# Moving the third plain tile of the first unit of block products

## The chip, the cores and the metric

The kernel runs on one core of one Trainium2 chip. The metric is the device time of one execution in microseconds, lower is better; times are medians over runs. Engines are named as in the profile: PE (TensorE), DVE (VectorE), ACT (ScalarE), POOL (GpSimd), SP (SyncE, here a queue of transfers), and PEld for the loading of PE's weights.

## The reference

Three stages follow one another, all in float32:

```
x = attention(q, k, v)              # 2 x 8 heads x 768 x 64 -> x: 1536 x 512
P = sinkhorn(exp(x @ w_gate))       # 8 rounds, P: 1536 x 8
for e in range(8):                  # dense mixture of experts, F = 1024
    out += P[:, e:e+1] * (relu(x @ w1[e]) @ w2[e])
out2 = routed mixture of experts(out)   # one expert of 8 for each row
```

The change lies in the second stage, the dense mixture.

## The kernel before

**Numbers in two parts.** Each float32 operand of a matmul is kept as two parts, `hi` (a cast, written by ACT) and `lo` (the rest, a subtraction on DVE). A product takes three matmuls: hi x hi, hi x lo, lo x hi.

**The dense stage.** An expert is cut into two halves of 512 features, `hx` = 0 to 15. The first two halves (`hx` 0 and 1) go the plain way in units of 384 rows: `mm1` (L597) makes the features and `mm2` (L624) adds one tile of 128 rows to its accumulator, in 12 matmuls of 512 columns; this is a plain tile. From `hx` = `FIRST` = 2 on, both layers are done as seven block products instead of eight on sets of 512 rows (`self.sets`, three for each `hx`). `first` (L747) gives the seven products of layer one, `s1` to `s7`, and `second` (L846) those of layer two, `z1` to `z7`, which use the features of the set before. So layer two runs one unit behind layer one. Each product is 12 matmuls of 256 columns at L708 (`multiply`), and yields twice, once ahead of each half.

**The order of a unit** is written by hand:

```python
TURNS = "s1 z1 s2 z7 z6 s6 s7 z5 s5 z2 z4 s3 z3 s4".split()
```

The first unit of block products (`hx` 2, set 0) has no layer two behind it (`behind` is None), so its z turns are free. Three plain tiles of `hx` 1 are still waiting then (rows 1152 to 1535, tiles 9, 10 and 11), and `pieces` puts them and some beats into the free turns. In what follows, tile A, B and C are the first, second and third of them; the unit after the first is called the second unit.

**Beats.** At every yield `steps` (L942) calls `beats` (L512) once. A beat first takes one step of every chain that is under way (`self.soon`) and then pops one entry of the list `self.later`. So the place of small work on DVE, ACT and POOL is counted in beats. A chain with None between its steps spreads them over beats. The engines run their instructions in the order in which they are issued here.

**The weights of layer two.** When no plain tile is left, `tiles` (inside `pieces`) issues `rescale` for tiles 9, 10 and 11 (L649 on POOL, then a store at L652 on SP) and calls `new_seconds(2)`. This fills `self.later` with, in order,

```
B11, sumT1, sumT3, T3, sumT2, T2, T1, B21, sumT4, T4, B22
```

each followed by a None, then one more None, and then four loads of the next layer-one weights (L466, on POOL's queue). So entry 0 is B11, entry 6 T3, entry 10 T2, entry 12 T1, entry 20 B22, and entries 23 to 26 are the loads. A `sum` entry is one DVE instruction (L575). Each other entry is the cast `hi` on ACT (L590) in its beat and the subtraction `lo` on DVE (L591) two beats later. Product z1 uses B11, z7 uses T3, z6 uses T2, z5 uses T1. The buffers of the raw weights number four, and the loads reuse them.

**Work behind the products.** Product s5 is followed by a copy of its PSUM bank X on ACT (L802), then on later beats an addition on DVE (L803), a relu and a cast on ACT, a subtraction on DVE. Product s3 adds to the same bank X, so its first matmul waits for that copy. After s3, DVE runs L809 and L810 at once and L818 and three subtractions (L743) on later beats; after s4, L840 at once, and L739, L837 and one L743 on later beats. After s2, DVE runs L782. Results of layer two leave through POOL as adding transfers to memory (L886).

**Transfers of SP.** The right-hand operands T of layer one are read back from memory into a ring of seven; after each of s6, s7, s5 and s4 the next one is fetched (L534, two transfers on SP's queue). SP's stores of `rescale` are in the same queue.

Of the kernel before, what the change touches and what calls it, by code (L numbers as in the profile page):

```python
# [387 lines left out]
class DenseMoe:  # L388
# [612 lines left out]
    def pieces(self, done, plain):  # L1001

        NG = self.NG
        self.seen = set()
        units = [(hx, g) for hx in range(self.FIRST) for g in range(NG)] + self.sets  # L1010
        waiting, behind = [], None
        soon = range(self.FULL + 1, self.LAST)

        def loads(which, hx):
            return [partial(self.load, which, hx, c) for c in range(4)]

        def new_seconds(hx):

            if hx <= self.FULL:
                for what in self.SECONDS:  # L1020
                    self.later += [partial(self.weights, 2, hx, what), None]
                self.later += [None] + loads(1, hx + 1)
            elif hx < self.LAST:
                for what in self.SECONDS_SOON:
                    if what is None:
                        self.later.append(None)
                    elif isinstance(what, int):
                        self.later.append(partial(self.load, 1, hx + 1, what))
                    else:
                        self.later.append(partial(self.weights, 2, hx, what))  # L1030
            else:
                for what in self.SECONDS:
                    self.later += [partial(self.weights, 2, hx, what), None]
                self.later += [None] + loads(1, hx + 1)

        def tiles(hx, n=1):

            for _ in range(min(n, len(waiting))):
                e, i, f = waiting.pop(0)
                yield  # L1040
                yield from f()
                if not waiting and (2, hx, 0) in self.raw:
                    if hx == self.FIRST:
                        for t in range(3 * NG - 3, 3 * NG):
                            self.rescale(t)
                        new_seconds(hx)
                    else:
                        self.later += [partial(self.split, 2, hx, c) for c in range(4)]

        for u, self.goal in self.opening():  # L1050
            yield u
        waiting = self.left
        for i, (hx, g) in enumerate(units):
            if i < NG - 1:
                continue
            n = hx + 1
            last = i + 1 == len(units) or units[i + 1] == (n, 0)
            if self.strassen(hx):
                self.blocks = {}
                todo = {**self.first(hx, g), **(behind or {})}  # L1060
                for k, turn in enumerate(self.TURNS):
                    if turn in todo:
                        for _ in todo[turn]():
                            yield i
                        if (hx, g) == (self.FIRST, 0) and k == 0:
                            for t in range(3 * NG - 3):
                                self.rescale(t)
                    elif turn in ("z1", "z7", "z6"):
                        for _ in tiles(hx):
                            yield i  # L1070
                    elif turn in ("z2", "z4"):
                        self.beats()
                        self.beats()
                    if last and n > self.LAST:
                        if turn in ("s7", "s5", "s3", "s4"):
                            self.split(1, n, ("s7", "s5", "s3", "s4").index(turn))
                    elif last:
                        for what in (self.FIRSTS_LATE if hx in soon else self.FIRSTS).get(turn, ()):
                            self.weights(1, n, what)
                    if last and hx == self.FULL:  # L1080
                        for c in {"s5": (0,), "z3": (1, 2)}.get(turn, ()):
                            self.load(2, n, c)
                        if turn == "s4":
                            self.later += [None, None, partial(self.load, 2, n, 3)]
                    elif last and turn == "s4":
                        self.later += [None] + loads(2, n)
                    if g == 0 and behind and turn == ("z1" if hx in soon else "z6"):
                        new_seconds(hx)
                behind = self.second(hx, g, self.blocks)
                continue  # L1090
            for c in range(4):
                yield i
                if g == 1 and n <= self.FIRST:
                    self.load(1, n, c)
                for _ in self.mm1(hx, g, c):
                    yield i
                if last and self.strassen(n):
                    for turn in (("s1", "s2", "s6", "s7"), ("s5",), ("s3",), ("s4",))[c]:
                        for what in self.FIRSTS[turn]:
                            self.weights(1, n, what)  # L1100
                    if c == 3:
                        self.later += loads(2, n)
                elif last:
                    self.split(1, n, c)
                    self.load(2, n, c)
                for _ in tiles(hx, 1 + (len(waiting) + c > 3)):
                    yield i
            waiting = self.tiles_of_group(hx, g)
        yield from self.rest(len(units), behind, loads, done, plain)
# [1248 lines left out]
```

## Time and profile before

| | |
|---|---|
| median of 3 runs | 1288.38 us (1287.43 to 1289.87) |
| the profiled execution, its own time | 1287.23 us |
| its span in the profile | 1285.5 us |
| mean granted clock of PE | 0.997 |
| busy PE, DVE, ACT, POOL | 99%, 69%, 61%, 29% of the span |

Times in the rows are microseconds from the start of the span. The span is the stretch from the first to the last instruction, and the time lies 1.73 us above it. PE is the engine that is busy nearly all the time. The first unit of block products runs on PE from 213.53 to 232.65 us, the second from 232.65 us on.

### The profile page before, as it was taken

To read this page: it belongs to the slowest core of one execution; us is meant where nothing else is said; L and a number is where in the kernel's file an instruction comes from. 1 tells how busy PE (TensorE), PEld (TensorE's weight loads), DVE (VectorE), ACT (ScalarE), POOL (GpSimd) and SP (SyncE) were. 2 spreads that over 40 slices of the span, in tenths; PEclk is the share of its full clock that TensorE was granted. 3 is DMA by queue.
4 is the path that set the end of the run, shared out by engine and by line. 5 is a ranking of instruction groups with operands and counts; after the bars stand their busy time and mean duration, and the time that the engine had idled before them with its cause. 6 is when DMAs were issued, how large, how long until landed. Compare 5 with 4: busy or idle time off the path is not lost.

```text
span 1285.5 us, 27044 instructions
## 1 busy us (share of the span) xinstructions
PE 1267.0 (99%) x10187; PEld 1194.1 (93%) x10187; DVE 885.4 (69%) x1724; ACT 782.5 (61%) x1601; POOL 376.6 (29%) x388
## 2 busy tenths in 40 slices
PE   7999999999999999999999999999999999999997
PEld 7888898999999999999999999999999978888886
DVE  7754596777778686777877777778697677514261
ACT  5764322667767676776776767767677635425361
POOL 6652005323324242333332323323122201211110
PEclk9999999999999999999999999999999999999999
DMA  9950237778889797988888989889897648123450
GB/s 224 195 123 10 91 120 274 198 193 184 191 189 194 197 201 172 218 171 224 165 211 185 199 191 185 190 189 199 194 213 177 144 150 303 58 73 134 150 182 23
DMA packets 172220, 221.20 MB, mean 172 GB/s; under 512 B 46927, under 2 KB 103279, under 8 KB 172080
## 3 DMA queue, kind: packets, MB, share of 16 engines
q1 hardware_dynamic: 119504, 146.20, 37.1%
q0 software_dynamic: 52576, 73.19, 33.3%
q8 instruction: 82, 1.34, 0.4%
q14 instruction: 58, 0.48, 0.1%
HBM read 163.76 MB, written 56.36 MB: 171 GB/s over the span
## 4 chain that ended last, share of the span: by engine, by line
PE 91%; DMA 3%; issue 2%; DVE 1%; ACT 1%; POOL 1%; POOLq 0%; SPq 0%; DVEq 0%; ACTq 0%
PE bank L708 62%; PE bank L1960 9%; PE bank L631 7%; PE bank L611 5%; DMA out_dram<-o,r_idxf 3%; PE bank L687 2%; PE bank L223 1%; PE bank L292 1%; PE bank L1989 1%; PE bank L279 1%; DMA kn<-in_k_dram 1%; PE bank L1236 0%; PE bank L1951 0%; PE bank L103 0%; ACT e L252 0%
## 5 line engine op out<-in xcount | busy, mean ns | idle before, releaser
L886 POOL DMA_DIRECT2D x2d<-acc x156 | 187.1, 1241 | 502.7 <-DVE lo L591 179.1
L708 PE MATMUL bank<-hi,hlo 128*128 128x256 f32 x748 | 211.5, 283 | 0.3 <-DVE hlo L743 0.3
L708 PE MATMUL bank<-lo,hhi 128*128 128x256 f32 x748 | 211.4, 283 | 0.0
L708 PE MATMUL bank<-hi,hhi 128*128 128x256 f32 x748 | 211.0, 282 | 0.0
L708 PE MATMUL bank<-Tlo,hi 128*128 128x256 f32 x640 | 181.0, 283 | 0.0
L708 PE MATMUL bank<-Thi,lo 128*128 128x256 f32 x640 | 180.7, 282 | 0.0
L708 PE MATMUL bank<-Thi,hi 128*128 128x256 f32 x640 | 180.1, 281 | 0.0
L708 PE MATMUL bank<-hi,acc 128*128 128x256 f32 x744 | 147.9, 282 | 0.0
L708 PEld LDWEIGHTS bank<-hi,hhi 128*128 128x128 f32 x748 | 142.4, 190 | 0.3 <-DVE Thi L906 0.2
L708 PEld LDWEIGHTS bank<-hi,hlo 128*128 128x128 f32 x748 | 141.8, 190 | 0.5 <-DVE hlo L743 0.5
L708 PEld LDWEIGHTS bank<-lo,hhi 128*128 128x128 f32 x748 | 141.8, 190 | 0.1
L708 PE MATMUL bank<-xhi,hi 128*128 128x256 f32 x480 | 134.9, 281 | 0.7 <-ACT t L802 0.7
L708 PE MATMUL bank<-xlo,hi 128*128 128x256 f32 x480 | 134.9, 281 | 0.0
L708 PE MATMUL bank<-xhi,lo 128*128 128x256 f32 x480 | 134.8, 281 | 0.0
L708 PEld LDWEIGHTS bank<-hi,acc 128*128 128x128 f32 x744 | 121.5, 190 | 0.0
L708 PEld LDWEIGHTS bank<-Thi,hi 128*128 128x128 f32 x640 | 121.1, 189 | 0.0
L708 PEld LDWEIGHTS bank<-Thi,lo 128*128 128x128 f32 x640 | 120.6, 188 | 0.0
L708 PEld LDWEIGHTS bank<-Tlo,hi 128*128 128x128 f32 x640 | 120.3, 188 | 0.0
L743 DVE TENSOR_TENSOR hlo<-t,hhi 128x512 fp32r<-128x512 f32 x160 | 107.9, 686 | 15.0 <-ACT hhi L735 13.5
L735 ACT CAST hhi<-t 128x512 fp32r<-128x512 f32 x160 | 97.8, 619 | 28.4 <-DVE t L837 21.9
L881 ACT ACTIVATE acc<-acc,P 128x256 f32<-128x256 f32 x234 | 104.7, 501 | 2.0 <-DVE acc L923 2.0
L708 PE MATMUL bank<-lo,acc 128*128 128x256 f32 x372 | 105.1, 283 | 0.0
(337 smaller groups left out, 3233.3 us busy)
## 6 DMA issues: line engine op xcount, KB each, us to landing
x2d<-acc POOLq DMA_DIRECT2D x163, 256.0 KB, 4.7
Thi<-td SPq DMA_DIRECT2D x160, 256.0 KB, 3.7
Tlo<-td SPq DMA_DIRECT2D x160, 256.0 KB, 4.2
raw<-in_moe_w_dram POOLq DMA_DIRECT2D x88, 256.0 KB, 5.8
raw<-in_moe_w_dram SPq DMA_DIRECT2D x20, 1024.0 KB, 5.9
raw<-in_moe_w_dram SPq DMA_DIRECT2D x56, 256.0 KB, 4.5
vw<-in_v_dram SPq DMA_DIRECT2D x32, 120.0 KB, 4.5
kn<-in_k_dram SPq DMA_DIRECT2D x8, 384.0 KB, 5.2
```

The source lines that it names most:

```text
L223: nc.tensor.matmul(self.sc[par][64 * hh:64 * hh + 64, j, slice(96, 120) if own else slice(0, 96)], qT[p, 64 * t:64 * t + 64], ks[p] if own ...
L279: nc.tensor.transpose(tr[0:120, j, :], an[:, 3 * par + j, :], self.ident)
L292: nc.tensor.matmul(o[64 * par:64 * par + 64, 128 * j + 64 * hh:128 * j + 64 * hh + 64], vw[:, t, par, :], aT[:, 3 * par + j, 64 * hh:64 * ...
L611: nc.tensor.matmul(ps, w[:, 128 * k:128 * k + 128], x[:, k], start=(n == 0), stop=(n == 11),)
L631: nc.tensor.matmul(ps, h, w, start=(n == 0), stop=(n == last))
L687: nc.tensor.matmul(ps, w[:, 128 * k:128 * k + 128], x[:, k], start=(n == 0), stop=(n == 11))
L708: self.nc.tensor.matmul(bank[:, 256 * f:256 * f + 256], x[:, o:o + 128], y[:, k], start=first and n == 1, stop=n == 12, skip_group_check=True,
L735: nc.scalar.copy(hi, src)
L743: nc.vector.tensor_tensor(out=lo, in0=src, in1=hi.bitcast(F32), op=ALU.subtract)
L881: nc.scalar.activation(out=out[:, s], in_=src[:, s], func=ACTF.Copy, scale=self.P[:, i, hx // 2:hx // 2 + 1],)
L886: nc.gpsimd.dma_start(out=self.sums[n:n + 256, 256 * dh:256 * dh + 256].rearrange("(c p) d -> p c d", p=128), in_=out.rearrange("p (c d) - ...
L1960: self.nc.tensor.matmul(ps, x[:, k], y[:, k], start=(n == 0), stop=(n == 12 * len(parts) - 1))
```

## The change

Tile C moves from turn z6, ahead of s6, to turn z4, between s5 and s3. The four extra beats, which stood together at z2 and z4 between s5 and s3, are now two at z6 (where tile C was) and two at z2, ahead of tile C. In the turns of the first unit:

```
before: s1 A s2 B C       s6 s7 s5 2+2 beats   s3 s4
after:  s1 A s2 B 2 beats s6 s7 s5 2 beats  C  s3 s4
```

With tile C, what its end sets off moves too: `rescale` of tiles 9 to 11 with its stores, and `new_seconds(2)`. In all other units every z turn holds a product, so nothing changes there.

```diff
@@ -1065,10 +1065,10 @@
                         if (hx, g) == (self.FIRST, 0) and k == 0:
                             for t in range(3 * NG - 3):
                                 self.rescale(t)
-                    elif turn in ("z1", "z7", "z6"):
+                    elif turn in ("z1", "z7", "z4"):
                         for _ in tiles(hx):
                             yield i
-                    elif turn in ("z2", "z4"):
+                    elif turn in ("z6", "z2"):
                         self.beats()
                         self.beats()
                     if last and n > self.LAST:
```

## Rows read from the trace of the kernel before

**Rows 1.** The page: busy time, share of the span and instructions of each engine.
```profile
PE 1267.0 (99%) x10187; PEld 1194.1 (93%) x10187; DVE 885.4 (69%) x1724; ACT 782.5 (61%) x1601; POOL 376.6 (29%) x388
```

**Rows 2.** Waits of PE, 200 to 300 us: total, times, longest.
```profile
PE bank L708 <- ACT t L802: 0.7, 1, 0.7
PE bank L708 <- DVE hlo L743: 0.3, 1, 0.3
```

**Rows 3.** Timeline of PE, first and second unit: start, duration, instruction, [idle before].
```profile
221.81 0.39 PE L631 MATMUL bank<-hi,hhi 128*128 128x512 f32 x1
...
224.53 0.28 PE L708 MATMUL bank<-Thi,hi 128*128 128x256 f32 x1
...
228.72 0.28 PE L708 MATMUL bank<-Thi,lo 128*128 128x256 f32 x1
229.67 0.39 PE L708 MATMUL bank<-xhi,hi 128*128 128x256 f32 x1 [0.68 <-ACT t L802]
229.89 0.28 PE L708 MATMUL bank<-xlo,hi 128*128 128x256 f32 x1
...
236.90 0.29 PE L708 MATMUL bank<-hi,hhi 128*128 128x256 f32 x1
...
238.34 0.28 PE L708 MATMUL bank<-hi,hhi 128*128 128x256 f32 x1
...
239.05 0.39 PE L708 MATMUL bank<-hi,hlo 128*128 128x256 f32 x1 [0.31 <-DVE hlo L743]
239.27 0.28 PE L708 MATMUL bank<-hi,hhi 128*128 128x256 f32 x1
...
240.35 0.28 PE L708 MATMUL bank<-Thi,hi 128*128 128x256 f32 x1
```

**Rows 4.** Timeline of DVE, first and second unit.
```profile
226.66 0.98 DVE L575 TENSOR_TENSOR raw<-raw 128x512 f32<-128x512 f32 x1
...
230.25 0.68 DVE L591 TENSOR_TENSOR lo<-raw,hi 128x512 fp32r<-128x512 f32 x1
...
232.30 0.68 DVE L809 SCALAR_TENSOR_TENSOR t<-bank,t 128x512 f32<-128x512 f32 x1
...
233.50 0.68 DVE L591 TENSOR_TENSOR lo<-s,hi 128x512 fp32r<-128x512 f32 x1
...
240.24 0.68 DVE L782 TENSOR_TENSOR t<-bank,t 128x512 f32<-128x512 f32 x1
```

**Rows 5.** Timeline of ACT, the copy of bank X behind s5.
```profile
229.03 0.59 ACT L802 COPY t<-bank 128x512 f32<-128x512 f32 x1 [2.28 <-PE bank L708]
```

**Rows 6.** Timeline of POOL, 205 to 290 us.
```profile
225.51 2.46 POOL L649 TENSOR_SCALAR acc<-acc,P 128x512 f32<-128x512 f32 x1 [1.16 <-DVE acc L638]
...
243.03 0.72 POOL L466 DMA_DIRECT2D raw<-in_moe_w_dram  x1 [3.96 <-DVE lo L591]
248.15 1.25 POOL L886 DMA_DIRECT2D x2d<-acc  x1 [4.40 <-DMA Thi<-td]
...
276.25 3.35 POOL L466 DMA_DIRECT2D raw<-in_moe_w_dram  x4
```

**Rows 7.** Timeline of SP's queue, the stores of `rescale`.
```profile
220.25 8.07 SPq L652 DMA_DIRECT2D x2d<-acc  x3
```

**Rows 8.** Timeline of DVE, third unit and after: sums of loaded weights.
```profile
255.46 0.68 DVE L575 TENSOR_TENSOR s<-raw 128x512 f32<-128x512 f32 x1
...
284.37 0.69 DVE L575 TENSOR_TENSOR raw<-raw 128x512 f32<-128x512 f32 x1 [0.75 <-DMA raw<-in_moe_w_dram]
```

**Rows 9.** Stretches: length, busy PE, PEld, DVE, ACT, POOL, clock, DMA, GB/s.
```profile
13.30:16.10 2.80, 0.07 (x3) 0.04 (x2) 2.69 (x16) 1.89 (x8) 1.07 (x1) 0.88 1.23 213
...
15.00:20.00 5.00, 3.91 (x36) 3.44 (x40) 2.91 (x15) 2.68 (x13) 3.79 (x4) 0.66 1.25 219
...
1277.00:1278.00 1.00, 0.41 (x2) 0.00 (x0) 0.00 (x0) 0.56 (x1) 0.00 (x0) 1.00 0.00 0
...
1281.00:1282.00 1.00, 0.00 (x0) 0.00 (x0) 0.00 (x0) 0.00 (x0) 0.00 (x0) 0.90 0.02 4
```

## The prediction

> **What bounds the kernel now.** I read the page first: PE is busy 99% of the span [rows 1], so time is won or lost only where PE waits or where a matmul is added, and this change adds none. Next the waits of PE around the first unit: between 200 and 300 us there are just two, 0.7 us for a copy on ACT and 0.3 us for a subtraction on DVE [rows 2]. The timeline of PE then shows where they lie [rows 3]. The first is in the first unit between s5 and s3: s5's last matmul starts at 228.72, s3's first should follow 0.12 later and starts at 229.67, and its second, due at 228.96, starts at 229.89. That is a loss of 0.93 us. It is the copy of bank X behind s5, which runs from 229.03 to 229.62 [rows 5]. The second is in z6 of the second unit: its third matmul starts at 239.05 and its fourth at 239.27 instead of 238.70, a loss of 0.57 us; the operand is the subtraction for block S2. Last the timeline of DVE: from L809 (232.30) to L782 (240.24) it runs 13 steps in 7.94 us, 0.61 us each, without a hole [rows 4]. In that stretch DVE is the engine that is behind, and PE lives from what was done earlier.
>
> **What the change gains.** Without the hole the end of s5, 228.84, becomes the end of tile C, because the same pieces stand before it. Tile C takes 2.72 us (221.81 to 224.53), so s5 ends at 226.12 and s3 begins at 228.84. The copy on ACT starts 0.19 us after the end of s5 (229.03 against 228.84) and takes 0.59, so it is done at 226.9, 1.9 us ahead of s3. The gain is 0.93 us. What hides the copy is tile C, which uses another bank. Everything on PE after it comes 0.93 us earlier unless something new is late.
>
> **What it delays.** `new_seconds` is called at the end of tile C. Before, 14 beats of the first unit followed it (s6, s7, s5 two each, four extra, s3 and s4 two each); now four follow (s3 and s4). So every entry of the list comes ten beats, or five products, later against the products that use it. Before, B11, sumT1 and sumT3 ran on DVE until 227.64 and T3's `lo` at 230.25 [rows 4], in time that DVE had free. Now B11 is cast at s3, its `lo` and sumT1 come at s4, sumT3 at the second unit's s1, T3's cast at z1 and its `lo` at s2, one product ahead of z7 that reads it; sumT2 comes at s2, T2's cast at z7 and its `lo` at z6, in the very product that reads it. So these six DVE steps move into the stretch in which DVE had no hole.
>
> The queue of DVE, written out in the new order, begins with L809, which waits for s3. With a product at 1.44 us (236.90 to 238.34) s3 ends at 230.28, and with about 0.2 us to the reader (as at the copy) L809 starts at 230.5. Behind it stand, in order: L810, B11 lo, sumT1, L818, L840, sumT3, three steps for S3, S1 and S2, L739, L837, T3 lo (the 12th), sumT2, L782, one step for S4, T2 lo (the 16th). B11's `lo`, two steps behind L809, is there at 232.4, ahead of z1 at 233.1. ACT's casts are done ahead of each of them: the latest is T2's, which can begin when sumT2 ends. At 0.61 us a step:
> - T3 lo starts at 230.5 + 12 x 0.61 = 237.83 and, with 0.68 of its own, is there at 238.51. z7 is due at 236.90 - 0.93 = 235.97, its second matmul, which reads T3 lo, at 236.09. It starts at 238.54, and the next one after 0.22 instead of 0.12, as after the other two holes. Loss 2.55 us; z7 ends at 239.96.
> - T2 lo starts at 230.5 + 16 x 0.61 = 240.28, is there at 240.96. The second matmul of z6 is due at 240.08 and starts at 240.99. Loss 1.01 us; z6 ends at 242.41.
> - The old hole in z6 goes, since S2's step now stands ahead of T3 lo: gain 0.57.
>
> Sum: -0.93 - 0.57 + 2.55 + 1.01 = +2.06 us. The same by position: z6 ended at 240.35 (the start of s6) and now ends at 242.41. After that T1 lo follows T2 lo with one step between, at about 242.2, and z5 reads it at 245.3; B21, T4 and B22 have more room. PE has no other wait up to 300 us [rows 2] that could take some of it back, so I keep the 2.06 us to the end.
>
> **The bounds of that sum.** It hangs on one number, the end of T2 lo. At 0.60 us a step (232.30 to 233.50 are two steps) it is 0.2 us earlier. The `rescale` of tile 11 moves with tile C to about 230.3 to 232.8 (2.46 us on POOL [rows 6]); the one DVE sum that ran beside it took 0.98 us instead of 0.68 [rows 4], and one such step here adds 0.3 us. From below, if the late operands cost nothing, the sum is -1.50. From above, 0.68 us for each of the 16 steps, the whole of one with nothing overlapped, gives 1.1 more, +3.2. I take 0.61, since the old stretch had the same mix.
>
> **What moves at no cost.** SP's queue: the three stores took their places at 220.25 to 228.3 [rows 7], ahead of the fetches behind s6, s7 and s5; now those fetches go first and the stores follow, the last after `rescale` at about 232.8, with the fetch behind s4 after it. Fetches run seven operands ahead and a unit uses four, so that fetch is not wanted before the second unit's s4, some 20 us later. `rescale` of tiles 9 and 10 still runs as soon as their sums are there. Nobody adds to these rows before the third set. The beats at z6 pop an empty list.
>
> **The loads.** The four loads of layer-one weights come at z2, z4 and s3 of the second unit, on POOL's queue, where they now stand behind and between L886. The first L886 started at 248.15 and would start at 250.2; with 0.7 to 0.9 us for a load and 1.2 for the next L886 between them the fourth load issues at about 254.1, against 243.03 before [rows 6]. The loads from 276.25 on, four in 3.35 us, show the delay to the data: the fourth issues at about 278.8, and the sum that waited for it started at 284.37 [rows 8], 5.5 us later. So it lands at 259.6, and the sum that reads it, at 255.46 before [rows 8], would come at 257.5 and now waits 2.1 us with DVE's queue behind it. Behind it stand L739, L837, a `lo` and L782 (2.4 us), then relu and cast on ACT (1.2) and the copy of z6's bank (0.6), which z5 needs: 264.6, and z5 is due at 265.4. I count nothing, with 0.8 us to spare.
>
> **Rivals.**
> - *The operands are in time* (15%): DVE would have T3 lo at 236.1, 2.4 us earlier than my queue. For it: DVE is busy only 69% of the span [rows 1], and it had holes in the first unit. Against: the holes lie before s3's end, and the order of issue forbids using them. Time -1.50 us, faster by 0.12%.
> - *The loads stall PE* (12%), the case on the slower side: the place is the sum of loaded weights in the third unit. It decides if the fourth load lands after 260.4; each microsecond beyond goes to z5. With one more L886 ahead of it and landing in 6 us it would be 1.7 us later than I reckon, 0.9 on PE, up to 2 if the transfers crowd. Time about +3.5 us, slower by 0.27%.
> - *The clock falls in z7's wait* (15%). At 13.4 us PE stopped for 2.73 us, the granted clock was 0.88 over 13.30 to 16.10 and 0.66 over 15 to 20, which is 3.4 us at the lower level, 1.2 GHz [rows 9]. Against it: behind dense matmuls PE ended at 1277.41, and the clock was full until about 1281.8, 4.4 us later. My wait is 2.4 us behind dense work, nearer in length to the first and in kind to the second. Of 3.4 us at half rate at most 1.7 is lost; part falls into z6's wait, so I take 1.2. Time +3.3 us, slower by 0.25%. [...]
> - *The forecast* (58%): +2.06 us, slower by 0.16%.
>
> **How the numbers follow.** Against the profiled execution, 1287.23, the forecast is 1289.3. It lies 1.15 below the median of the runs, so against the median, 1288.38, it is 1290.4, which I give. About 0.2%, 2.6 us, is what a measurement can tell from no change; the three runs alone spread over 2.44. The range takes in the bounds above and the rivals: from 1287.6 (most of the case without a cost is left out) to 1293.0 (loads and clock are in). The forecast and the clock case lie close to the bound of 0.2% on either side: of the forecast's 58% I give 13 to slower by over 0.2%, of the clock's 15 eleven, of the loads' 12 eleven. Slower 0.35, faster 0.02, same 0.63.
>
> **What would show it.** Right: no wait of PE for L802 between s5 and s3; a wait of 2.2 to 2.6 us in z7 and of 0.7 to 1.1 in z6, both for L591 on DVE; no wait for L743 in z6; L591 for T3 ending near 238.5; the fourth load issued near 254 and the sum of loaded weights waiting for it with PE not stopping in the third unit. Wrong: no wait in z7 (then -1.50), a granted clock under 1 at 236 to 244, a wait of PE near 265 us, or a change of PE's pace far from these units.

## The result, and the profile after

The changed kernel took 1296.78 us (median of 6 runs, 1294.70 to 1300.49) against 1288.34 of the kernel before (6 runs): the recorded ratio is 1.0060, 95% interval 1.0048 to 1.0072. Timed a second time, beside other runs of the kernel before, it was 1294.81 against 1288.96, 1.0037 (1.0026 to 1.0048). The ratios of the medians themselves, 1.0066 and 1.0045, lie inside these intervals. It is slower, by 0.4 to 0.7%, and the medians lie 8.4 and 5.9 us above where 2.06 were forecast.

The profiled execution is the slowest of the six, 1300.49 us with a span of 1298.8. All its times in the units of block products stand 3.29 us later to begin with: the first unit starts at 216.82 instead of 213.53, because of the opening, of which more below.

First the waits of PE, 200 to 300 us, in the kernel after (answers to [rows 2]):

```profile
PE bank L708 <- DVE lo L591: 2.7, 2, 2.3
PE bank L708 <- ACT acc L900: 1.7, 1, 1.7
PE bank L708 <- DVE acc L906: 0.3, 1, 0.3
```

Both waits of before are gone, and others stand there, for three instructions. The timeline of PE says where (answers to [rows 3]; start, duration, instruction, idle before):

```profile
216.82 0.28 PE L708 MATMUL bank<-xhi,hi 128*128 128x256 f32 x1
...
232.17 0.28 PE L708 MATMUL bank<-xhi,hi 128*128 128x256 f32 x1
...
239.30 0.30 PE L708 MATMUL bank<-hi,hhi 128*128 128x256 f32 x1
241.88 0.39 PE L708 MATMUL bank<-lo,hhi 128*128 128x256 f32 x1 [2.29 <-DVE lo L591]
...
244.29 0.58 PE L708 MATMUL bank<-lo,hhi 128*128 128x256 f32 x1 [0.40 <-DVE lo L591]
...
246.67 0.28 PE L708 MATMUL bank<-Thi,hi 128*128 128x256 f32 x1
...
269.49 0.28 PE L708 MATMUL bank<-Thi,lo 128*128 128x256 f32 x1
271.51 0.39 PE L708 MATMUL bank<-hi,hhi 128*128 128x256 f32 x1 [1.74 <-ACT acc L900]
...
276.36 0.39 PE L708 MATMUL bank<-hi,acc 128*128 128x256 f32 x1 [0.26 <-DVE acc L906]
```

Product s3 starts at 232.17 without a wait. In the second unit the second matmul of z7 comes 2.58 us after the first (239.30 to 241.88), and the second of z6 starts at 244.29. In the third unit z5 waits at 271.51. DVE and ACT (answers to [rows 4, 5, 8]):

```profile
229.61 0.59 ACT L802 COPY t<-bank 128x512 f32<-128x512 f32 x1 [2.29 <-PE bank L708]
```

```profile
233.81 0.69 DVE L809 SCALAR_TENSOR_TENSOR t<-bank,t 128x512 f32<-128x512 f32 x1 [0.24 <-PE bank L708]
...
241.15 0.68 DVE L591 TENSOR_TENSOR lo<-raw,hi 128x512 fp32r<-128x512 f32 x1
...
243.55 0.68 DVE L591 TENSOR_TENSOR lo<-s,hi 128x512 fp32r<-128x512 f32 x1
...
266.44 0.69 DVE L575 TENSOR_TENSOR s<-raw 128x512 f32<-128x512 f32 x1 [4.75 <-DMA raw<-in_moe_w_dram]
```

T3's subtraction ends at 241.83 and T2's at 244.23, right ahead of the two matmuls that waited. The sum of loaded weights waits 4.75 us for a transfer. POOL shows that transfer's place (answers to [rows 6]):

```profile
254.32 1.49 POOL L886 DMA_DIRECT2D x2d<-acc  x1 [19.09 <-ACT acc L881]
255.32 1.99 POOL L466 DMA_DIRECT2D raw<-in_moe_w_dram  x2
256.83 1.76 POOL L886 DMA_DIRECT2D x2d<-acc  x1
257.59 2.44 POOL L466 DMA_DIRECT2D raw<-in_moe_w_dram  x2
```

And the stretches with the granted clock (answers to [rows 9]; length, busy PE, PEld, DVE, ACT, POOL, clock, DMA, GB/s):

```profile
239.00:242.00 3.00, 0.71 (x6) 0.51 (x6) 2.96 (x6) 1.26 (x3) 0.00 (x0) 1.00 0.00 0
...
243.10:246.50 3.40, 3.00 (x15) 2.71 (x14) 2.43 (x4) 1.74 (x3) 0.00 (x0) 0.50 0.00 0
246.50:250.00 3.50, 3.50 (x31) 3.50 (x30) 1.30 (x3) 2.31 (x4) 0.00 (x0) 1.00 0.18 43
```

PE idles in the first of them at full clock; in the second the clock is at 0.50, 1.2 GHz, for about 3.4 us, and z6's matmuls follow one another every 0.21 us instead of 0.12.

**Where the time went.** Both traces hold the same 10187 matmuls on PE, so the n-th of one can be set against the n-th of the other, outside the first unit, whose order differs. The table gives the lag of a kernel behind the first profile of before: the opening is the lag at the start of the first unit (213.53 us before), and the others are what was added from there on, at the start of the second unit, after z6 with the clock up again (245 us before), and behind the third unit (300 us before).

| kernel, profile | opening | start of unit 2 | after z6 | behind unit 3 | last matmul |
|---|---|---|---|---|---|
| changed, first | +3.29 | -0.89 | +2.86 | +5.40 | +9.92 |
| changed, second | +4.09 | -0.89 | +2.75 | +5.09 | +4.69 |
| changed, third | +3.26 | -0.89 | +2.73 | +4.95 | +5.52 |
| before, second | +2.31 | 0.00 | -0.01 | -0.01 | -0.36 |
| before, third | +2.48 | 0.00 | -0.01 | -0.01 | -0.03 |
| loads early | +3.16 | -0.89 | +4.47 | +4.47 | +4.36 |
| list late, tile C not moved | +2.24 | 0.00 | +3.69 | +7.17 | +6.85 |
| all early, first | +0.35 | -0.89 | -1.15 | -1.15 | -1.49 |
| all early, second | +2.26 | -0.89 | -1.17 | -1.17 | +3.99 |
| sums early | -0.16 | -0.89 | +0.11 | +2.21 | +3.57 |
| fill in front of z7 | +1.74 | -0.89 | +1.92 | +4.25 | +3.98 |
| loads on SP | +2.81 | -0.89 | +2.85 | +2.85 | +6.02 |

From 300 us to about 940 us nothing is added in any of them. Near 955 us sums early gains 1.7 us of lag, the third profile of the changed kernel 0.9, the third of before 0.3 and the others under 0.1. The change itself is the 5.0 to 5.4 us of the first three units, 0.4%.

### The profile page after: what moved, and what is told of

Its sections match the earlier page's. It is cut to its first block, busy times and chain, and to the rows that moved or that the text cites. A ratio compares the mean times of both kernels' runs of the same rounds, so it can differ in the third digit from the quotient of the medians.

```text
span 1298.8 us, 27046 instructions
## 1 busy us (share of the span) xinstructions
PE 1272.7 (98%) x10187; PEld 1198.9 (92%) x10187; DVE 886.2 (68%) x1724; ACT 782.9 (60%) x1601; POOL 377.5 (29%) x388
## 4 chain that ended last, share of the span: by engine, by line
PE 88%; DMA 5%; issue 2%; DVE 2%; ACT 1%; POOLq 0%; SPq 0%; POOL 0%; ACTq 0%; DVEq 0%
PE bank L708 61%; PE bank L1960 9%; PE bank L631 6%; PE bank L611 5%; DMA out_dram<-o,r_idxf 3%; DMA raw<-in_moe_w_dram 1%; PE bank L292 1%; PE bank L687 1%; PE bank L223 1%; PE bank L1989 1%; PE bank L279 1%; DMA kn<-in_k_dram 1%; DMA qn<-in_q_dram 1%; PE bank L103 0%; PE bank L1236 0%
## 5 line engine op out<-in xcount | busy, mean ns | idle before, releaser
L886 POOL DMA_DIRECT2D x2d<-acc x156 | 190.9, 1274 | 514.8 <-DVE lo L591 194.1
L743 DVE TENSOR_TENSOR hlo<-t,hhi 128x512 fp32r<-128x512 f32 x160 | 107.6, 684 | 16.2 <-ACT hhi L735 15.0
```

The source lines that it names most:

```text
L743: nc.vector.tensor_tensor(out=lo, in0=src, in1=hi.bitcast(F32), op=ALU.subtract)
L886: nc.gpsimd.dma_start(out=self.sums[n:n + 256, 256 * dh:256 * dh + 256].rearrange("(c p) d -> p c d", p=128), in_=out.rearrange("p (c d) - ...
```

## The experiments

The theory after the result: the gain between s5 and s3 is there; the list that comes ten beats later costs more than it, in three places: DVE's queue ahead of z7 and z6, the clock that falls behind z7's wait, and the loads on POOL's queue that stall the third unit. The rivals: the place of tile C itself costs, with `rescale` and the stores behind it; or the change also lengthens the opening and the stretch near 1090 us.

**The changed kernel and the kernel before again** (`r1_after_again`, `r2_before_again`, `r3_after_third`, `r4_before_third`, no edit).

> The changed kernel once more. Its first profile was 13.2 us longer in span: 5.4 us around the first three units of block products, 3.3 in the opening attention stretch and 4.5 near 1090 us, where the code is the same as before. Theory A (only the 5.4 us belong to the change, the rest is chance): again about +5.4 us between 213 and 300 us, something else in the other two stretches, time about +5 to +9. Theory B (the change brings all three): +3.3 and +4.5 come again, time about +13.

> The kernel before once more, for the stretches that the change does not touch. In the first profile of it the clock was at its lower level for 3.4 us at 15 us; in two profiles of the changed kernel and one of its variants it was so for 6.8 us at 31 us and the opening took 3.2 to 4.1 us longer, in two other variants 6.8 us at 15 us and 0.4 to 2.2 longer. Theory A: the opening differs between executions of one kernel, so this profile differs from the first by some tenths to 4 us before 100 us, and by nothing between 213 and 300 us. Theory B (the opening is longer in the changed kernel only): the same as the first profile within 0.5 us.

> The changed kernel a third time, for the stretches where its code is that of before. Its two profiles so far had openings 3.3 and 4.1 us longer than the first profile of before, the variants of it between -0.2 and +3.2, the kernel before itself +2.3 in its second profile. Theory A (chance): an opening anywhere between -0.2 and +4.1, and about +5 us between 213 and 300 us again. Theory B (the change lengthens the opening): +3 to +4 again.

> The kernel before a third time. Theory A (chance): an opening anywhere between -0.2 and +4.1 us against its first profile. Theory B: under 2.5 us as in its other two. Nothing changes between 213 and 300 us under either.

The three units repeat within half a microsecond: +5.40, +5.09, +4.95 for the changed kernel, nothing for the kernel before. The opening does not: the kernel before itself was 2.31 and 2.48 us longer in its second and third profile, so its first profile was one of the short ones. The stretch near 1090 us added 4.7 us in the first profile of the changed kernel and nothing in the second and third. So that part is chance. The trace of that first profile shows what happened there: ACT waited 1.60 us for a load of weights, its copy L1452 came late, PE waited for the copy, and the clock fell behind the wait (0.52 over 1095 to 1100 us).

```profile
PE bank L1459 <- ACT r_xt L1452: 1.4, 1, 1.4
```

The same wait and the same fall stand in the second profile of all early (+5.4 us there) and in that of loads on SP (+3.4). In the opening the three changed profiles (+3.3 to +4.1) all lie above the three of before (0 to +2.5), and variants lie from -0.2 to +3.2; the waits of PE there, of up to 4.1 us, for loads of q and k, for DVE's L239 or for nothing that the profile shows, differ from profile to profile, and so does the time at the lower clock (3.4 us in the first profile of before, 6.8 in the first of the changed kernel). Whether the changed kernel's opening is longer on average these profiles can't tell.

**The ten beats alone** (`e2_list_late`): the kernel before, tile C in its old place.

```diff
+            if hx == self.FIRST:
+                self.later += [None] * 10
             if hx <= self.FULL:
                 for what in self.SECONDS:
```

> The kernel before, tile C in its old place, with ten empty entries ahead of the list of layer-two weights, so that each entry comes on the beat of the changed kernel. Theory A (the ten beats are the whole cost): waits of about 2.3 us in z7 and 0.4 in z6 for L591, the wait in the third unit, and the wait between s5 and s3 as before: about 0.9 us more than the changed kernel between 213 and 300 us, +6.3 against the kernel before. Rival (the place of tile C itself, with the rescale and SP's queue behind it, costs): no more than +2 us against before.

1.0050 (1.0030 to 1.0070), and the waits of PE, 200 to 320 us:

```profile
PE bank L708 <- DVE lo L591: 3.0, 2, 2.3
PE bank L708 <- ACT acc L900: 1.7, 1, 1.7
PE bank L708 <- ACT t L802: 0.7, 1, 0.7
PE bank L708 <- ACT hi L590: 0.5, 1, 0.5
```

The waits in z7, in z6 and for L900 in the third unit are there without the move, and the old one for L802 beside them. The sum, +7.17, is 0.9 above the +6.3 expected, and the excess lies in the third unit: it added 3.5 us instead of 2.2 to 2.5, because here the clock fell behind its wait (0.62 over 271.0 to 275.5). In the second unit the clock stayed up, which saved about as much as another delay cost: L809 stood behind a subtraction of s5's chain, T3's subtraction ended 1.8 us later than in the changed kernel, openings taken off, and z7 first waited 0.5 us for a cast. So the list's place is the cost, not tile C's.

**The sums early** (`e4_sums_early`): only three DVE steps leave the queue.

```diff
                     elif turn in ("z6", "z2"):
+                        if turn == "z6":
+                            for what in ("sumT1", "sumT3", "sumT2"):
+                                self.weights(2, hx, what)
                         self.beats()
```

(In the list their entries are None.)

> The changed kernel with only sumT1, sumT3 and sumT2 moved to turn z6 of the first unit, the rest of the list on its beats. Theory A (the place in DVE's queue sets the wait): T3's subtraction comes two steps or 1.2 us earlier, the wait in z7 is 1.1 us instead of 2.3; T2's three steps or 1.8 us earlier, the wait in z6 at most 0.3; the third unit's waits for the late loads stay at about 2 us. About +2.6 us against before if the clock stays up, time 2 to 3 us less than the changed kernel. Rival (T3 waits for its cast or for the raw weights, not for DVE's queue): the wait in z7 stays at 2.3.

1.0030 (1.0013 to 1.0046). Waits of PE, 200 to 320 us:

```profile
PE bank L708 <- ACT acc L900: 1.3, 1, 1.3
PE bank L708 <- DVE lo L591: 1.1, 1, 1.1
PE bank L708 <- DVE acc L906: 0.3, 1, 0.3
```

Two steps less ahead of T3 take the wait in z7 from 2.3 to 1.1 us, as the queue says, and z6 does not wait at all. The clock stays up. The sum after z6 is +0.11; the third unit adds 2.1, about as in the changed kernel.

**PE kept at work where it waited** (`e5_fill`).

```diff
+                    if (hx, g, turn) == (self.FIRST, 1, "z7"):
+                        fill, w = self.psum("b", [128, 512]), self.w[2, hx, "B11"][0]
+                        for n in range(10):
+                            self.nc.tensor.matmul(
+                                fill, w[:, 0:128], w, start=(n == 0), stop=(n == 9)
+                            )
```

> The changed kernel with ten extra matmuls of 512 columns (2.3 us) between s2 and z7 of the second unit, into a PSUM bank that nobody reads, so that PE works where it waited. Theory A (PE's wait in z7 lets the clock fall to its lower level for 3.4 us or more, which costs 0.9 us or more in z6): z7 still starts its second matmul when T3's subtraction is done, the clock stays at its upper level around 243 us, and the stretch from z7 to the second unit's s6 is 0.9 us shorter than in the changed kernel, in spite of the extra work. Rival (the clock falls for another reason, or the slow matmuls in z6 are waits): the clock falls as before and nothing is gained.

1.0032 (1.0021 to 1.0043). PE around z7 and z6:

```profile
237.75 2.46 PE L1065 MATMUL bank<-hi 128*128 128x512 f32 x10
240.05 0.28 PE L708 MATMUL bank<-hi,hhi 128*128 128x256 f32 x1
240.34 0.39 PE L708 MATMUL bank<-lo,hhi 128*128 128x256 f32 x1
...
242.75 0.39 PE L708 MATMUL bank<-lo,hhi 128*128 128x256 f32 x1 [0.72 <-DVE lo L591]
```

```profile
243.10:246.50 3.40, 3.40 (x31) 3.40 (x30) 2.03 (x4) 1.92 (x4) 0.00 (x0) 1.00 0.00 0
```

With ten matmuls more the second unit ends 0.8 to 0.9 us earlier (+1.92 after z6 instead of +2.73 to +2.86): the clock did not fall. Here z7 and z6 cost what the two subtractions cost and nothing else, and +1.92 is the forecast of +2.06 within 0.14 us. The third unit still added 2.3 us: the loads are late without the clock's fall too.

**The loads early** (`e1_loads_early`): entries 9, 11, 19 and 23 of the list, as soon as their buffers are read.

```diff
+            if hx == self.FIRST:
+                at = len(self.later)
+                for what in self.SECONDS:
+                    self.later += [partial(self.weights, 2, hx, what), None]
+                self.later += [None] + loads(1, hx + 1)[3:]
+                for n, c in ((9, 0), (11, 1), (19, 2)):
+                    self.later[at + n] = partial(self.load, 1, hx + 1, c)
-            if hx <= self.FULL:
+            elif hx <= self.FULL:
```

> The changed kernel with only the four loads of the next layer-one weights taken from the end of the list to entries 9, 11, 19 and 23, as soon as their buffers are read; everything else at its place. Theory A (the sum of loaded weights in the third unit waits 4.75 us because the loads stand behind and between the adding transfers on POOL's queue): the wait of DVE goes, PE's waits of 1.7 and 0.3 us in the third unit go, time 2.5 us less than the changed kernel; the waits in z7 and z6 stay. Rival (the load is late because DVE reads its buffers late, or transfers are slow anyway): the wait stays within 1 us of what it was.

1.0016 (1.0005 to 1.0027); the median, 1291.66, lies 3.1 us below the changed kernel's, timed beside the same runs of before. The third unit adds nothing, and the only waits left, 200 to 320 us, are those in z7 and z6 for L591:

```profile
PE bank L708 <- DVE lo L591: 2.8, 2, 2.3
```

The profiled execution shows another thing: the same wait of 2.3 us was followed by a low clock of twice the length.

```profile
243.10:246.50 3.40, 2.85 (x15) 2.56 (x14) 2.30 (x4) 1.62 (x3) 0.00 (x0) 0.51 0.21 77
246.50:250.00 3.50, 3.50 (x18) 3.50 (x18) 1.29 (x2) 1.63 (x4) 0.10 (x1) 0.50 0.00 0
```

After z6 it is at +4.47, so the clock cost 2.5 us here (4.47 - 1.92) and 0.8 to 0.9 in the three profiles of the changed kernel. Why it stayed down twice as long, no run here shows.

**The loads on another queue** (`e6_loads_sp`), on the same late beats.

```diff
-            (nc.sync if hx == self.FIRST or hx > self.FULL else nc.gpsimd).dma_start(
+            (nc.sync if hx == self.FIRST or hx > self.FULL or (which, hx) == (1, self.FIRST + 1) else nc.gpsimd).dma_start(
```

> The changed kernel with the four loads of the third half's layer-one weights on SP's queue instead of POOL's, on the same beats. Theory A (the loads are late because on POOL they stand behind adding transfers that wait for ACT, and share that queue's transfers): they issue by 256 us and land in about 4.6, the sum of loaded weights does not wait more than 0.5 us and PE's waits of 1.7 and 0.3 us in the third unit go, 2.4 us less than the changed kernel. Rival (ten beats late is too late on any queue): the sum still waits 2 us or more and PE waits with it.

1.0028 (1.0012 to 1.0044). The sum of loaded weights does not wait, nor does the third unit:

```profile
261.11 0.68 DVE L575 TENSOR_TENSOR s<-raw 128x512 f32<-128x512 f32 x1
```

Time from issue to landing of the four loads, on SP's queue here (three of the four are traced to their landing) and on POOL's in the kernel after (us, shortest, median, longest):

```profile
DMA to landing us min/median/max: 3.8/5.0/5.3
```

```profile
DMA to landing us min/median/max: 6.2/7.0/8.0
```

On SP they also issued earlier, the last at 254.50, against 258.34 on POOL behind L886, which waited for ACT. So ten beats late is not too late by itself; the queue made it so, by the later issue and the slower landing together. The median, 1292.56, lies 2.3 us below the changed kernel's second one, as expected, though that was timed beside other runs of before.

**All of it early** (`e3_all_early`, and `e7_all_early_again` without an edit): tile C as in the change, the three sums at turn z6 as above, and the list of the first half as

```python
"B11", None, "T3", None, "T2", 0, "T1", 1, "sumT4", None, "B21", None, "T4", 2, "B22", None, None, 3
```

where a number is the load of that part.

> The changed kernel with tile C between s5 and s3, but the three sums that need no buffer (sumT1, sumT3, sumT2) at turn z6, the list in the order B11, T3, T2, T1, sumT4, B21, T4, B22 and the loads among them at entries 5, 7, 13 and 17. Theory A: no wait of PE between s5 and s3, in z7, in z6 or in the third unit, the clock stays at its upper level there, about -1.5 us against the kernel before (0.12%, at the edge of what can be told). Rival (tile C's new place costs by itself): a wait stays or a new one comes, 0 to +4 us.

> The version with tile C between s5 and s3, the three sums at turn z6, the shorter list and the early loads, timed a second time, since its first interval, 0.9981 to 1.0002, touched 1. By its trace it is 1.15 us (0.09%) ahead between 213 and 300 us. Theory A: 0.998 to 1.000 again. Rival (nothing is left of the gain): 1.000 or more.

0.9991 (0.9981 to 1.0002) and 0.9995 (0.9985 to 1.0004). PE has one wait left between 200 and 320 us in both profiles, and the trace is 1.15 and 1.17 us ahead behind the third unit:

```profile
PE bank L708 <- ACT acc L900: 0.2, 1, 0.2
```

The gain, 0.09%, stands in both traces, and the timing can't tell it from nothing. This is the version that has tile C's new place without its cost; no version here beats the kernel before by a measurable amount.

The medians bear the table out. Against the runs of before that were timed with them they lie +5.9 us for the changed kernel (second timing; 5.1 in its trace behind the third unit), +7.2 for the list late (7.2), +2.7 for the sums early (2.2), +3.8 for the fill (4.3), +2.9 for the loads on SP (2.9) and -1.2 and -0.5 for all of it early (-1.2). The loads early lie at +2.7 where their trace has +4.5; that trace is the one with the low clock of twice the length. The first timing of the changed kernel, at +8.4, is the one that its trace behind the third unit, +5.4, doesn't cover.

## Why the prediction was wrong

- **What the change gains**: right. 0.93 us were forecast, 0.89 are there in every kernel with the move. The copy ran behind s5, with tile C over it.
- **What it delays, the DVE queue**: right to a few hundredths of a microsecond. T3 lo was put at 238.51 and T2 lo at 240.96; less the opening's 3.29 they ended at 238.54 and 240.94. With the clock held up by the fill the sum came out at +1.92 for +2.06.
- **The loads**: this step failed. "I count nothing, with 0.8 us to spare" rested on a fourth load that issues at 254.1 and lands 5.5 us later. The issue was right: in the kernel with the fill, where the clock stayed up, the fourth load issued at 255.85, 254.11 less that opening. The landing was wrong: it took 7.8 us there, and 8.0 in the changed kernel, where the issue was also 0.95 us late (258.34, or 255.05 less the opening), nearly all of it by the clock's fall before. So the sum that was put at 259.6 came at 263.15 (266.44 - 3.29), 3.5 us later, the spare 0.8 was used up, and the third unit lost 2.2 to 2.5 us (2.3 with the fill). The 5.5 us came from the four loads at 276.25, which follow one L886 and stand one behind the other (their trace has 5.8 for the last of them, the other two profiles of before 5.5 and 6.9); here two L886 stood around the first two loads, and the last two came behind both; the fourth took 7.6 to 8.0 us in all six profiles with this order. That the adding transfers between them made the landing longer is the nearest reading; no run took these away alone. The mechanism stood among the rivals, and its place and its point of decision were right.
- **The clock**: the second step that failed, put at nothing in the forecast and among the rivals with 15%. It fell in all three profiles of the changed kernel, behind z7's wait, and cost 0.8 to 0.9 us; I had put 1.2. I weighed it on two rows, a wait of 2.73 us with a fall and the end of the kernel, after which the clock stayed up for 4.4 us [rows 9], and called the wait to come nearer in kind to the second, behind dense matmuls. That difference does not hold: PE was busy for 3.30 of the 3.30 us ahead of the first row's wait too (10.0 to 13.3 us). A wait of 2.29 us was enough. The Trainium skill, "TensorE: Matmul & The Clock Gate", section "Why this matters for your kernels", warns of idle gaps between bursts of matmuls, after which the clock goes back to its lower level, and the gaps that it names are longer than this one. The trace has the fall behind the shorter wait, at 0.50 over 243.10 to 246.50, and the measurement decides.
- **How the numbers follow**: the rivals were treated as exclusive, and the range reached to one of them. They came together with the forecast: +1.92 for the queue, 0.8 to 0.9 for the clock and 2.2 to 2.5 for the loads make the 5.0 to 5.4 of the traces. With the prediction's own prices, 2.06, 1.2 and 2 over 1288.4, the upper end would have been 1293.6, still short of both medians.
- What is left, 3 us of the first comparison and less than 1 of the second, was not found in the three units. It lies in stretches where the code is the same, in the opening and near 955 and 1090 us, as far as the profiles show; which of them made up the 3 us of the first median stays open. The profile on which the sum was based had the shortest opening but one of all thirteen.

Of the signs named beforehand these came: no wait for L802, 2.29 us in z7 (2.2 to 2.6 forecast), none for L743. In z6 it was 0.40 (0.7 to 1.1 forecast), because the clock had already slowed the matmuls ahead of it; at full clock, in the kernel with the fill, it was 0.72. Those that would make it wrong came too: a clock under 1 at 236 to 244 (243.10 to 246.50, less the opening's 3.29) and a wait of PE near 265, at 271.51 or 268.2 less the opening.

## What to carry to other kernels

When a piece of work is moved to cover a hole, ask first what its end triggers. Here a tile's end opened the list that feeds the next layer, and ten beats of delay there cost six times the hole (6 us for 0.9). The order of DVE's queue, written out with the trace's own pitch, gave the ends of both subtractions to a few hundredths of a microsecond, and POOL's order gave the issue of the fourth load; a transfer's time to landing did not carry over, since it was taken from loads with other transfers around them. Rivals that work in different places add up, so a range has to hold their sum.

## What the runs showed of the hardware

- A wait of 2.3 us of PE between dense matmuls was followed by the lower clock in five of the six profiles that had it, for about 3.4 us in four of them and 6.8 us in the fifth (loads early). The price was 0.8 to 0.9 us where it was down for 3.4, and 2.5 us in the fifth.
- The length of the wait alone did not decide. After 1.7 us in the third unit the clock fell in the list late (1.73) and stayed up in the changed kernel's first profile (1.74); it stayed up after 1.3 to 1.6 us there in four other profiles, and after 1.1 us in z7 (sums early). Near 1090 us it fell after 1.4 us (changed, first), 1.7 (loads on SP) and 2.0 (all early, second).
- The one of the four loads on POOL's queue that the trace of before follows to its landing took 5.8 us, with no adding transfer beside it (6.3 in the second profile of before). In the changed kernel, among adding transfers, they took 6.2 to 8.0 us, median 7.0. Their pace on POOL hardly changed: from the first L886 to the fourth load it was 4.02 us, where 3.9 were reckoned.
- The opening, in which PE waits among others for loads of q and k, differs by up to 4.2 us between executions with the same code there (-0.16 to +4.09 against the first profile), more than the effect that was to be measured.
